# The order of the first loads and of the output stage's work in a gated pair of linear attentions

## The chip, the cores and the metric

The kernel runs on one core of a Trainium2 chip. A core has a matrix engine (TensorE, called PE in the profile), a vector engine (VectorE, DVE), an activation engine (ScalarE, ACT), a general engine (GpSimd, POOL) and a sequencer that mostly issues transfers (SyncE, SP). The engines run on their own and wait for one another through semaphores. PE reads the on-chip memory SBUF and writes the accumulation memory PSUM; transfers between the chip's main memory and SBUF (DMA) are issued by SP or ACT. The metric is the device time of one execution in microseconds (us), as the median of several runs.

## The reference

Two linear attentions with 32 heads of width 20 work on the same input x (2048 rows, 640 columns, bf16) with weights of their own, and a gate mixes the two outputs row by row:

```python
x = A_x
g = sigmoid((x * gate_w).sum(-1, keepdims=True))
a = attention(x, A_wqkv, A_wo)
b = attention(x, B_wqkv, B_wo)
return g * a + (1 - g) * b

def attention(x, wqkv, wo):            # per head: q, k, v are 2048 x 20
    q, k, v = split(x @ wqkv)
    pq, pk = phi(q), phi(k)            # phi(t) = (t + 1 if t > 0 else exp(t)) + 1e-6
    kv, z = pk.T @ v, pk.sum(rows)
    o = (pq @ kv) / (pq @ z + 1e-6)
    return merge_heads(o) @ wo
```

## The kernel before

In the text that follows A and B are the two attentions. The kernel never forms v. For each attention it computes k = x wk in 16 chunks of 128 rows (`k_chunk`, line 227), applies phi (`phi`, lines 214 to 223), and computes q transposed (`q_block`, `q_unit`, lines 274 to 295). Then G = xᵀ phi(k) gives kv as a product with wv, and kv times wo gives a matrix M of 640 by 640 (`g_all`, `kv_mm`, `m_mm`); the scaled phi(q) times M is one attention's output. M goes through main memory (`m_dram`) to change its layout. The sum over A and B of these products in the output stage is written as a two by two block product with seven products in place of eight, on sums and differences of blocks: the sums of the phi(q) blocks are `p_sums` (three kinds, 1, 2 and 4, for each of four parts of 256 rows) and those of M's blocks `m_sum` (0 to 3), all of them on DVE at line 519.

**The start.** The weights wkA come in five row blocks c of 128 by 640, 160 KB each (`load_wk`, line 120). The first two row blocks of x, 160 KB each, are loaded as they are (`load_x`, line 114) and turned by PE against an identity matrix (`x_transpose`, line 206), with DVE copying each from PSUM to xT in two pieces (line 209). The other rows of x are turned by the transfer itself (`x_turned`, line 117), and come after the first loads in SP's queue, with wqA between them (line 130). SP issues the first x block and wkA's blocks 0, 2 and 4; ACT issues gate_w, the second x block and blocks 1 and 3. ACT loads its table for the exponential when the first one is due (the row of line 214 named ACT_TABLE_LOAD).

POOL builds constants (identity, masks, spreading matrices; lines 135 to 156). PE runs seven products of 512 columns of ones into an unused bank (`warm`, line 163). The gate's logit is a 641st column of wkA: gate_w is loaded as 5 rows of 128 (`grow`), turned by PE (line 165), copied by DVE (`gsb`, line 167) and put by POOL into column 640 of each block of wkA (line 169, five copies). The products of a k chunk come in two halves of the columns; half 0 has 320 columns, half 1 has 321 with the gate's. `k_first` starts the first two chunks block by block: for each of the blocks 0, 1 and 2 both chunks with both halves, then blocks 3 and 4 of each chunk. POOL also clears R and fills parts of it from I16 (lines 686 to 691); this is used much later.

**The output stage.** Each of eight `Pair` objects i makes the output rows of row blocks i and i + 8. Its products p1 to p7 are five PE instructions of 320 columns each (`prod`, line 575). p1 and p5 go first for all pairs, in PSUM banks x and z, and ACT copies them into the memory of xn (lines 605, 609). p2 has the banks w and y; p6, p7 and p4 use bank x in this order: ACT copies p6's result (line 628), p7 accumulates on it, DVE adds that to an output tile, p4 accumulates further, DVE adds again. p3 has bank z. u25 (DVE) makes v out of p6's copy and p5; c11 (DVE) makes an output part of p2 and p1. DVE's additions are all at line 580, stores of finished rows at line 595, and the tiles for output rows are four in number. Where a product accumulates on a bank that DVE still has to read, PE waits.

**What sets the order.** Parts under `manual_schedule` run in the order of the program text on each engine; the rest is ordered by a planner. Every engine takes its own instructions strictly in order, and SP and ACT issue their transfers in the order of their instruction streams. In the kernel before, the first loads, the constants, the warm-ups and the gate column stand outside `manual_schedule`, `k_first` and the whole output stage inside.

Of the kernel before, what the change touches and what calls it, by code (L numbers as in the profile page):

```python
# [31 lines left out]
def kernel(  # L32
# [66 lines left out]
    lift = persist.tile([P, 1], FP32, name="lift")  # L99
# [5 lines left out]


    nc.vector.memset(ones[:], 1.0)
    nc.vector.memset(lift[:], 1.0 + EPS)
    wk = [None, None]
    wv = [None, None]  # L110
    wq = [None, None]
# [16 lines left out]
    x_turned(2 * P, HB)  # L128
    wq[0] = wpool.tile([P, DT, D], BF16, tag="wq", name="wqA")
    nc.sync.dma_start(out=wq[0][:], in_=wq_dram[0][:, :, 0:D])  # L130
    for n in range(1, NB):
        x_turned(n * HB, (n + 1) * HB)


    make_identity(nc, ident[:])
    for r in range(4):
        rows = slice(32 * r, 32 * r + 32)
        nc.gpsimd.tensor_copy(out=I4[rows], in_=ident[rows, rows])
    nc.gpsimd.tensor_copy(
        out=spread[:].rearrange("p (h t) -> p h t", t=TW), in_=I4[:, :, None].to_broadcast([P, H, TW])  # L140
    )
    nc.gpsimd.tensor_tensor(
        out=I16[0:2 * ST], in0=ident[0:2 * ST, 0:ST], in1=ident[0:2 * ST, ST:2 * ST], op=ALU.add
    )
    nc.gpsimd.memset(maskE[:], 1.0)
    for sign, base in ((1, 0), (-1, Dh - 1)):
        nc.gpsimd.affine_select(
            out=maskE[:], in_=maskE[:], pattern=[[-sign * Dh, WB[0] // Dh], [0, Dh]],
            compare_op=ALU.is_ge, fill=0.0, base=base, channel_multiplier=sign,
        )  # L150
    nc.gpsimd.memset(headE[:], 1.0)
    for sign, base in ((1, 0), (-1, TW - 1)):
        nc.gpsimd.affine_select(
            out=headE[:], in_=headE[:], pattern=[[-sign * TW, H]],
            compare_op=ALU.is_ge, fill=0.0, base=base, channel_multiplier=sign,
        )


    raw = ps_raw("warm", 3)
    warm = raw.bitcast(FP32).rearrange("p (b n) -> p b n", b=2)  # L160
    one_l, one_r = [nc.const_aps.tensor(1.0, [P, n], BF16) for n in (P, HB)]
    for k in range(7):
        nc.tensor.matmul(warm[:, 0, :], lhsT=one_l, rhs=one_r, start=True, stop=True)  # L163
    gcol = raw[:, 2 * HB:2 * HB + DT]
    nc.tensor.transpose(out=gcol, in_=grow, identity=ident[0:DT, 0:DT])
    gsb = work.tile([P, DT], BF16, tag="rT", name="gsb")
    nc.vector.tensor_copy(out=gsb[:], in_=gcol)
    for c in range(DT):
        nc.gpsimd.tensor_copy(out=wk[0][:, c, D:D + 1], in_=gsb[:, c:c + 1])

    def by_group(dst, lhsT, src, h):

# [31 lines left out]
    def x_transpose(i, pt, cuts=(0, DT)):  # L204
        for c in range(DT):
            nc.tensor.transpose(out=pt[:, c * P:(c + 1) * P], in_=xn[:, i, c * P:(c + 1) * P], identity=ident[:])
        src = pt[:, 0:D].rearrange("p (c n) -> p c n", c=DT)
        for lo, hi in zip(cuts, cuts[1:]):
            nc.vector.tensor_copy(out=xT[:, lo:hi, i * P:(i + 1) * P], in_=src[:, lo:hi])  # L209

    def phi(dst, src, n, lifted=False, side=None):

        e = work.tile([P, src.shape[1], n], BF16, tag="e", name="e", bufs=3)
        nc.scalar.activation(out=e[:], in_=src, func=ACT.Exp)  # L214
        if side is not None:
            side()
        if lifted:
            nc.scalar.activation(out=dst, in_=src, func=ACT.Identity, bias=lift[:])
# [462 lines left out]


    with tc.manual_schedule():
        k_first()
    turn[0] = 2
    nc.gpsimd.memset(R[:, :, 0:2, :], 0.0)
# [31 lines left out]
    with tc.manual_schedule():  # L718
# [35 lines left out]
        with late_pool("mid") as mid:  # L754
# [110 lines left out]
```

## Time and profile before

| | |
|---|---|
| median of 3 runs | 187.31 us (187.2 to 188.5) |
| profiled execution | 187.03 us, of which 185.3 us from the first to the last instruction (span) |
| PE busy | 181.4 us, 1338 products |
| DVE busy | 149.0 us |
| ACT busy | 78.6 us |
| POOL busy | 6.0 us |
| transferred | 17.59 MB, mean 95 GB/s |
| granted TensorE clock | 1.00 in the whole span |

All times in the text count from the start of the span unless they are whole executions. A PE row's length contains the time until the last result is in PSUM; the distance between the starts of two products tells the pace. An engine with a high busy share is not yet the bound: the chain of work that ended last tells which engine's work, or which wait, the end hangs on. A bracket at the end of a timeline row is the idle time of that engine before the row, and what ended it, as far as the semaphores tell.

### The profile page before, as it was taken

What the parts mean: (1) busy time and instruction counts of PE and PEld (TensorE: products, weight loads), DVE (VectorE), ACT (ScalarE), POOL (GpSimd) and SP (SyncE); (2) the same over time, 40 slices, a digit from 0 to 9 for tenths busy, and PEclk for the clock granted to TensorE, in tenths of its full rate; (3) what the DMA queues carried; (4) which work ended last, traced back from release to release, by engine and by line L of the source; (5) the groups of instructions that cost most, each with busy time, mean ns of one, the idle gap of its engine ahead of it and who ended that gap; (6) DMA issues with size and microseconds to landing.
All of it is one profiled execution on the core that took longest, in us unless ns stands there. A gap on an engine that the chain in (4) does not pass through costs nothing.

```text
span 185.3 us, 3375 instructions
## 1 busy us (share of the span) xinstructions
PE 181.4 (98%) x1338; PEld 121.6 (66%) x1338; DVE 149.0 (80%) x236; ACT 78.6 (42%) x132; POOL 6.0 (3%) x30
## 2 busy tenths in 40 slices
PE   8999999999999999999999999999999999999993
PEld 3666657755576677877765555576778777677762
DVE  0387869899999999799889998739699986978863
ACT  2345555557951501367664577431501863111010
POOL 6400000010000000000000000000000000000000
PEclk9999999999999999999999999999999999999999
DMA  5999998041140000011115000000533570023224
GB/s 166 332 240 165 308 372 189 6 132 46 19 162 0 0 4 0 0 36 34 55 45 189 4 0 0 0 4 0 177 89 92 175 182 3 35 106 110 108 83 131
DMA packets 21022, 17.59 MB, mean 95 GB/s; under 512 B 9998, under 2 KB 20750, under 8 KB 21006
## 3 DMA queue, kind: packets, MB, share of 16 engines
q1 hardware_dynamic: 20276, 16.72, 32.3%
q10 hardware_dynamic: 730, 0.66, 1.0%
q8 instruction: 10, 0.16, 0.4%
q14 instruction: 6, 0.05, 0.1%
HBM read 10.81 MB, written 4.26 MB: 81 GB/s over the span
## 4 chain that ended last, share of the span: by engine, by line
PE 97%; DVE 1%; issue 0%; ACT 0%
PE gs L351 17%; PE kA L227 12%; PE kB L227 12%; PE qB L274 12%; PE ox L575 11%; PE qA L274 6%; PE oz L575 6%; PE qA L285 5%; PE gB L324 2%; PE gA L324 2%; PE ow L575 2%; PE warm L163 2%; PE qA L295 1%; PE s L476 1%; PE mA L476 1%; PE kvA L446 1%
## 5 line engine op out<-in xcount | busy, mean ns | idle before, releaser
L227 PEld LDWEIGHTS <-xT 128*128 128x128 bf16 x320 | 31.1, 98 | 12.7 <-DVE xT L209 0.4
L219 DVE TENSOR_SCALAR e<-e 128x640 bf16<-128x640 bf16 (+2 forms) x53 | 18.9, 356 | 8.5 <-ACT e L214 7.9
L227 PE MATMUL kB<-wkB,xT 128*128 128x320 bf16 x160 | 23.0, 299 | 0.0
L227 PE MATMUL kA<-wkA,xT 128*128 128x320 bf16 (+1 forms) x160 | 22.6, 302 | 0.0
L274 PE MATMUL qB<-xT,wqB 128*128 128x512 bf16 x100 | 21.8, 379 | 0.0
L214 ACT ACTIVATE e<-kB 128x640 bf16<-128x640 f32 x16 | 11.3, 703 | 18.8 <-PE kB L227 17.5
L274 PEld LDWEIGHTS <-wqB 128*128 128x128 bf16 x100 | 11.7, 117 | 9.8 <-issue 0.2
L214 ACT ACTIVATE e<-kA 128x640 bf16<-128x640 f32 x16 | 11.2, 704 | 12.5 <-PE kA L227 12.5
L223 DVE SCALAR_TENSOR_TENSOR pk<-kA,e 128x640 bf16<-128x640 f32 x16 | 13.2, 825 | 2.1
L223 DVE SCALAR_TENSOR_TENSOR pk<-kB,e 128x640 bf16<-128x640 f32 x16 | 13.2, 825 | 1.7
L214 ACT ACTIVATE e<-qB 128x1024 bf16<-128x1024 f32 x10 | 10.2, 1023 | 8.7 <-PE qB L274 8.4
L214 ACT ACTIVATE e<-qA 128x1024 bf16<-128x1024 f32 (+1 forms) x11 | 10.4, 946 | 8.1 <-PE qA L285 5.1
L628 ACT COPY u<-ox 128x320 f32<-128x320 f32 x8 | 3.4, 425 | 20.2 <-PE ox L575 20.2
L351 PEld LDWEIGHTS <-S 128*128 128x128 bf16 x96 | 9.4, 98 | 3.6
L351 PEld LDWEIGHTS <-xn 128*128 128x128 bf16 x96 | 9.1, 98 | 4.0 <-issue 0.4
L274 PE MATMUL qA<-xT,wqA 128*128 128x512 bf16 x50 | 11.0, 379 | 0.0
L575 PEld LDWEIGHTS <-xT 128*128 128x128 bf16 x85 | 8.1, 98 | 3.2 <-issue 0.3
L575 PEld LDWEIGHTS <-pqTB 128*128 128x128 bf16 x80 | 7.8, 98 | 3.4 <-issue 0.2
L575 PEld LDWEIGHTS <-pqTA 128*128 128x128 bf16 x80 | 7.7, 98 | 3.1 <-DVE pqTA L519 0.3
L351 PE MATMUL gs<-pk,xn 128*128 128x320 bf16 x64 | 9.4, 300 | 0.0
L223 DVE SCALAR_TENSOR_TENSOR pqTB<-qB,e 128x1024 bf16<-128x1024 f32 x7 | 8.6, 1225 | 0.7
L274 PEld LDWEIGHTS <-wqA 128*128 128x128 bf16 x50 | 5.9, 117 | 4.8
(138 smaller groups left out, 287.0 us busy)
## 6 DMA issues: line engine op xcount, KB each, us to landing
out_dram<-osb SPq DMA_DIRECT2D x14, 160.0 KB, 1.8
xn<-in_A_x_dram SPq DMA_DIRECT2D x3, 640.0 KB, 5.6
wqA<-in_A_wqkv_dram SPq DMA_DIRECT2D x1, 800.0 KB, 5.1
wvA<-in_A_wqkv_dram SPq DMA_DIRECT2D x1, 800.0 KB, 10.1
wkB<-in_B_wqkv_dram SPq DMA_DIRECT2D x1, 800.0 KB, 4.8
wqB<-in_B_wqkv_dram SPq DMA_DIRECT2D x1, 800.0 KB, 4.5
MA<-mA_dram SPq DMA_DIRECT2D x1, 800.0 KB, 4.5
wvB<-in_B_wqkv_dram SPq DMA_DIRECT2D x1, 800.0 KB, 4.6
```

The source lines that it names most:

```text
L163: nc.tensor.matmul(warm[:, 0, :], lhsT=one_l, rhs=one_r, start=True, stop=True)
L214: nc.scalar.activation(out=e[:], in_=src, func=ACT.Exp)
L219: nc.vector.tensor_scalar(e[:], e[:], 1.0, EPS, op0=ALU.min, op1=ALU.add)
L223: nc.vector.scalar_tensor_tensor(out=dst, in0=src, scalar=1.0 + EPS, in1=e[:], op0=ALU.add, op1=ALU.max)
L227: nc.tensor.matmul(pt[:, hf, 0:w], lhsT=xT[:, c, i * P:(i + 1) * P], rhs=wk[b][:, c, hf * HF:hf * HF + w], start=(c == 0), stop=(c == DT - 1),
L274: nc.tensor.matmul(pt[:, u, :], lhsT=mixed(wq[b][:, c, :], m), rhs=xT[:, c, n * HB:(n + 1) * HB], start=(c == 0), stop=(c == DT - 1),)
L285: nc.tensor.matmul(pt[:, u, :], lhsT=mixed(wq[b][:, c, :], m + u), rhs=xT[:, c, n * HB:(n + 1) * HB], start=(c == 0), stop=(c == DT - 1),)
L324: nc.tensor.matmul(pt[:, hf, 0:HF], lhsT=xn[:, i, c * P:(c + 1) * P], rhs=pk[:, i, hf * HF:(hf + 1) * HF], start=(i == 0), stop=(i == ST - 1),
L351: nc.tensor.matmul(pt[:, n, 0:HF], lhsT=left[:, i, n * P:(n + 1) * P], rhs=right[:, i, :], start=(first and i == 0), stop=(i == hc - 1), s ...
L476: nc.tensor.matmul(dst[:w, 0:HF], lhsT=KVA[:w, k, 0:w], rhs=wo_sb[b][:w, k, n * HF:(n + 1) * HF], start=True, stop=True,)
L575: nc.tensor.matmul(dst, lhsT=left[:, c, r0:r0 + P], rhs=right[:, c, :], start=(first and c == 0), stop=(c == DT - 1), skip_group_check=not ...
L628: nc.scalar.copy(out=self.u6[:], in_=self.at("x"))
```

## The change

Four things are edited at the start. The second x block is loaded by SP, behind the first; wkA's blocks 0, 1 and 2 follow on SP, and blocks 3 and 4 are issued by ACT. ACT's queue now holds gate_w, then an exponential of one column (into a new second column of `lift`), for which the table is loaded, then the two blocks. The warm-ups are five products of 512 columns and two of 128. The gate column (transpose, DVE copy, POOL copies) comes after the turning of both x blocks, and within a chunk the products go by half first: half 0 of blocks 0 and 1, half 1 of both; then the other chunk; then block 2; then blocks 3 and 4. The loads and the constants are called inside `manual_schedule`; the clearing and filling of R stays outside it, and in the resulting order of POOL's instructions it stands between the constants, ahead of the five gate copies, where it stood behind them before.

In the output stage p1 of pairs 4 and 5 goes between p5 of pairs 1, 2 and 3; the sums 2 and 4 of a third part of rows are made before the inner loop instead of in it; m_sum(3) follows m_sum(2) directly, ahead of the c11 additions; and p3 of pair 6 stands between p7 of pair 6 and p6 of pair 7, where it was the product after p7 of pair 7. What PE computes in the two stages is the same, apart from the warm-ups.

```diff
-    nc.scalar.dma_start(out=grow, in_=gate_w.rearrange("(c p) -> c p", p=P))
-    load_x(nc.sync, 0)
-    load_x(nc.scalar, 1)
-    for c, eng in enumerate((nc.sync, nc.scalar, nc.sync, nc.scalar, nc.sync)):
-        load_wk(eng, c, c + 1)
...
+    def first_loads():
+
+        nc.scalar.dma_start(out=grow, in_=gate_w.rearrange("(c p) -> c p", p=P))
+        nc.scalar.activation(out=lift[:, 1:2], in_=lift[:, 0:1], func=ACT.Exp)
+        for i in range(2):
+            load_x(nc.sync, i)
+        for c in range(DT):
+            load_wk(nc.sync if c < 3 else nc.scalar, c, c + 1)
+        x_turned(2 * P, HB)
+        nc.sync.dma_start(out=wq[0][:], in_=wq_dram[0][:, :, 0:D])
+        for n in range(1, NB):
+            x_turned(n * HB, (n + 1) * HB)
...
-    for k in range(7):
-        nc.tensor.matmul(warm[:, 0, :], lhsT=one_l, rhs=one_r, start=True, stop=True)
...
+    def warm_up(n, w):
+        for k in range(n):
+            nc.tensor.matmul(warm[:, 0, 0:w], lhsT=one_l, rhs=one_r[:, 0:w], start=True, stop=True)
+
+    def gate_column():
+        nc.tensor.transpose(out=gcol, in_=grow, identity=ident[0:DT, 0:DT])
+        gsb = work.tile([P, DT], BF16, tag="rT", name="gsb")
+        nc.vector.tensor_copy(out=gsb[:], in_=gcol)
+        for c in range(DT):
+            nc.gpsimd.tensor_copy(out=wk[0][:, c, D:D + 1], in_=gsb[:, c:c + 1])
...
-        for i in range(2):
-            x_transpose(i, raw[i], (0, 2, DT))
-
-        def part(i, cs):
-            for c in cs:
-                for hf in range(2):
-                    k_mm(0, i, c, pts[i], hf)
-
-        for c in range(3):
-            for i in range(2):
-                part(i, (c,))
+        warm_up(5, HB)
+        warm_up(2, P)
+        x_transpose(0, raw[0], (0, 2, DT))
+        x_transpose(1, raw[1], (0, 2, DT))
+        gate_column()
+
+        def part(i, cs):
+            for hf in range(2):
+                for c in cs:
+                    k_mm(0, i, c, pts[i], hf)
+
+        part(0, (0, 1))
+        part(1, (0, 1))
+        for i in range(2):
+            part(i, (2,))
         for i in range(2):
             part(i, (3, 4))
             k_done(0, i, pts[i])
...
     with tc.manual_schedule():
+        first_loads()
+        constants()
         k_first()
...
-        for i in range(1, 4):
-            pairs[i].p5()
+        pairs[1].p5()
         for n in (2, 3):
             p_sums(part[n], (1,))
-        for i in range(4, half):
-            pairs[i].p1()
+        for i in (4, 6):
+            for k in range(2):
+                pairs[i + k].p1()
+                if i == 4:
+                    pairs[2 + k].p5()
         for i in range(4, half):
             pairs[i].p5()
-        for n in range(2):
+        for n in range(3):
             p_sums(part[n], (2, 4))
...
-        m_sum(1)
-        m_sum(2)
+        for k in (1, 2, 3):
+            m_sum(k)
...
-        m_sum(3)
-        later = {0: (2, (2,)), 1: (2, (4,)), 2: (3, (2,)), 3: (3, (4,))}
         ahead = {1: 4, 3: 5, 5: 6}
+        later = {1: 2, 3: 4}
         for i in range(half - 1):
             p, after = pairs[i:i + 2]
             p.p7()
             if i in ahead:
                 pairs[ahead[i]].p2()
                 pairs[ahead[i]].c11()
-            if i < half - 2:
-                p.p3()
+            p.p3()
             after.p6()
             after.u25()
             p.p4()
             if i in later:
-                p_sums(part[later[i][0]], later[i][1])
-        p, after = pairs[half - 2:]
+                p_sums(part[3], (later[i],))
         after.p7()
-        p.p3()
         after.p2()
         after.c11()
         after.p4()
         after.p3()
```

More of the change, by code (lines that the diff above doesn't have):

```diff
@@ L98 @@
     m_dram = [scratch.tile([D, D], BF16, name=f"m{b}_dram") for b in "AB"]
-    lift = persist.tile([P, 1], FP32, name="lift")
+    lift = persist.tile([P, 2], FP32, name="lift")
     TM = [persist.tile([P, DT, HF], BF16, name="TM0")] + [None] * 3
@@ L107 @@
     nc.vector.memset(ones[:], 1.0)
-    nc.vector.memset(lift[:], 1.0 + EPS)
+    nc.vector.memset(lift[:, 0:1], 1.0 + EPS)
     wk = [None, None]
@@ L122 @@
     grow, logitT = R[0:DT, 0, 2, 0:P], R[:, 0, 1, 0:P]
-    nc.scalar.dma_start(out=grow, in_=gate_w.rearrange("(c p) -> c p", p=P))
-    load_x(nc.sync, 0)
-    load_x(nc.scalar, 1)
-    for c, eng in enumerate((nc.sync, nc.scalar, nc.sync, nc.scalar, nc.sync)):
-        load_wk(eng, c, c + 1)
-    x_turned(2 * P, HB)
-    wq[0] = wpool.tile([P, DT, D], BF16, tag="wq", name="wqA")
-    nc.sync.dma_start(out=wq[0][:], in_=wq_dram[0][:, :, 0:D])
-    for n in range(1, NB):
-        x_turned(n * HB, (n + 1) * HB)
@@ L135 @@
[L135 to L149, printed above, removed]
-        )
@@ L151 @@
[L151 to L155, printed above, removed]
-        )
+    wq[0] = wpool.tile([P, DT, D], BF16, tag="wq", name="wqA")
+    def first_loads():
[9 more added lines that the diff above has]
+            x_turned(n * HB, (n + 1) * HB)
@@ new lines, in constants @@
+    def constants():
+        make_identity(nc, ident[:])
+        for r in range(4):
+            rows = slice(32 * r, 32 * r + 32)
+            nc.gpsimd.tensor_copy(out=I4[rows], in_=ident[rows, rows])
+        nc.gpsimd.tensor_copy(
+            out=spread[:].rearrange("p (h t) -> p h t", t=TW), in_=I4[:, :, None].to_broadcast([P, H, TW])
+        )
+        nc.gpsimd.tensor_tensor(
+            out=I16[0:2 * ST], in0=ident[0:2 * ST, 0:ST], in1=ident[0:2 * ST, ST:2 * ST], op=ALU.add
+        )
+        nc.gpsimd.memset(maskE[:], 1.0)
+        for sign, base in ((1, 0), (-1, Dh - 1)):
+            nc.gpsimd.affine_select(
+                out=maskE[:], in_=maskE[:], pattern=[[-sign * Dh, WB[0] // Dh], [0, Dh]],
+                compare_op=ALU.is_ge, fill=0.0, base=base, channel_multiplier=sign,
+            )
+        nc.gpsimd.memset(headE[:], 1.0)
+        for sign, base in ((1, 0), (-1, TW - 1)):
+            nc.gpsimd.affine_select(
+                out=headE[:], in_=headE[:], pattern=[[-sign * TW, H]],
+                compare_op=ALU.is_ge, fill=0.0, base=base, channel_multiplier=sign,
+            )
@@ L161 @@
     one_l, one_r = [nc.const_aps.tensor(1.0, [P, n], BF16) for n in (P, HB)]
-    for k in range(7):
-        nc.tensor.matmul(warm[:, 0, :], lhsT=one_l, rhs=one_r, start=True, stop=True)
     gcol = raw[:, 2 * HB:2 * HB + DT]
[L165 to L169, printed above, removed]
+    def warm_up(n, w):
[7 more added lines that the diff above has]
+            nc.gpsimd.tensor_copy(out=wk[0][:, c, D:D + 1], in_=gsb[:, c:c + 1])
     def by_group(dst, lhsT, src, h):
@@ L217, in phi @@
         if lifted:
-            nc.scalar.activation(out=dst, in_=src, func=ACT.Identity, bias=lift[:])
+            nc.scalar.activation(out=dst, in_=src, func=ACT.Identity, bias=lift[:, 0:1])
         nc.vector.tensor_scalar(e[:], e[:], 1.0, EPS, op0=ALU.min, op1=ALU.add)
```

## The prediction

> **What bounds it now.** I read the page first: engines, then the chain that ended last.
>
> ```profile
> PE 181.4 (98%) x1338; PEld 121.6 (66%) x1338; DVE 149.0 (80%) x236; ACT 78.6 (42%) x132; POOL 6.0 (3%) x30
> ...
> PE 97%; DVE 1%; issue 0%; ACT 0%
> ```
>
> TensorE (PE) is busy for 181.4 of 185.3 us and is 97% of the chain. The change removes no product of the calculation, so it can only win where PE works on nothing useful or waits: the first 6 us, a few stalls in the output stage, and the tail. Next the timeline of the first 16 us (start, length, engine, line, operation, and in brackets the idle time before it):
>
> ```profile
> 0.84 3.15 PE L163 MATMUL warm<-const-bfloat16-1.0 128*128 128x512 bf16 x7 [0.84 <-PEq L849]
> ...
> 3.61 0.20 POOL L153 TENSOR_SCALAR_AFFINE_SELECT headE<-headE 128x32 bf16<-128x32 bf16 x1
> ...
> 4.03 1.27 PE L206 MATMUL xt<-ident,xn 128*128 128x128 bf16 x10
> 4.14 0.16 DVE L167 COPY gsb<-warm 128x5 bf16<-128x5 bf16 x1 [3.16 <-PE warm L165]
> 4.37 0.66 POOL L169 COPY wkA<-gsb 128x1 bf16<-128x1 bf16 x5 [0.55 <-DVE gsb L167]
> 4.78 1.11 DVE L209 COPY xT<-xt 128x256 bf16<-128x256 bf16 x4 [0.48 <-PE xt L206]
> ...
> 4.96 0.95 POOL L686 MEMSET R<- 128x1024 bf16 x1
> ...
> 5.68 5.02 PEld L227 LDWEIGHTS <-xT 128*128 128x128 bf16 x38 [0.42 <-DVE xT L209]
> 5.97 0.98 POOL L691 COPY R<-I 32x128 bf16<-32x128 bf16 x4
> ```
>
> Warm-ups fill PE to 4.0 us, the ten transposes of x take 0.11 us each (4.03 to 5.13), and the first products of wkA start at 5.13. The third of them waits for VectorE's (DVE's) last copies of the transposed x (0.42 us before 5.68). My anchor is the fifth product: in narrow windows six start before 6.20, and the one still running at 6.20 began at 5.97. From there PE takes 0.136 us a product without a gap. Whatever moves that fifth product moves the end.
>
> The same view of the output stage shows the stalls there, as gaps before weight loads (PEld) and as the DVE operation that was late:
>
> ```profile
> 147.68 6.63 PEld L575 LDWEIGHTS <-pqTA 128*128 128x128 bf16 x50 [0.28 <-DVE pqTA L519]
> ...
> 158.67 0.98 DVE L519 TENSOR_TENSOR TM<-MB,TM 128x1600 bf16<-128x1600 bf16 x1
> ...
> 159.57 0.48 DVE L580 TENSOR_TENSOR osb<-ox,xn 128x320 bf16<-128x320 f32 x1
> ...
> 160.11 0.50 PEld L575 LDWEIGHTS <-pqTB 128*128 128x128 bf16 x4 [0.23 <-issue]
> ...
> 176.90 0.98 DVE L580 TENSOR_TENSOR osb<-ox,xn 128x320 bf16<-128x320 f32 x2
> ...
> 177.44 0.50 PEld L575 LDWEIGHTS <-xT 128*128 128x128 bf16 x4 [0.29 <-issue]
> ```
>
> Five products of 320 columns take 0.68 us (chain of waits). Measured against that, PE lost 0.11 us at 147.6, 0.18 at 159.9 to 160.1, 0.10 at 166.3 and 0.25 at 177.2 to 177.4: 0.64 us in all.
>
> **The start, part by part.** *Warm-ups.* Seven of 512 columns become five of 512 and two of 128: at 0.43 and 0.11 us each here, that is 0.86 - 0.22 = 0.64 us less, and PE is free at 0.84 + 2.3 = 3.1 instead of about 3.8. The first x block lands at 0.81 + 2.3 = 3.1, so its transposes start about 0.9 us earlier.
>
> *Gate column.* This is the step that decides. The gate's transpose (L165) and its DVE copy move behind the ten transposes and the four xT copies. By the instruction order, POOL's five copies into wkA (L169) move behind the memset of R and the four R copies, which stood after them before. POOL worked without a break on constants until 3.61 + 0.20 = 3.81; with 0.95 and 0.98 us put ahead, the gate copies cannot start before 5.74, and waits between dependent POOL operations, now interleaved differently, may make it 6.0. The first copy lasts 0.19 us; DVE to POOL took 0.07 us from end to start, so PE may go on at 6.0 to 6.25. What waits: the new order of parts gives half 0, blocks 0 and 1, then half 1 (321 columns, the last one being the gate), so two products can run early and the third waits for POOL. Behind it stands PE's whole queue. The DVE route says nearly the same: transposes of the second x end near 5.1, two copies of 0.3 us and the 0.16 us copy end near 5.9. The third product at 6.1 puts the fifth at 6.4, against 5.97: **+0.40 us** (0.3 to 0.55). The stall that goes (0.42 at 5.68) is inside this. The warm-ups' 0.64 us are thus used up waiting.
>
> *Loads.* The second x moves from ScalarE (ACT) to second place on SP; blocks 0, 1, 2 of wkA follow on SP; blocks 3 and 4 go to ACT behind gate_w's issue (to 1.38), the table load (1.28) and a one-column Exp. The trace has no such Exp: at least the 0.15 us of a one-column copy, at most the 0.70 of a 640-column Exp; I take 0.2, as the width is the copy's. Block 3 is then issued at 2.9 and block 4 at 3.4. Landing took 3.1 to 4.0 us after issue for the wkA blocks: 6.0 to 6.9 and 6.5 to 7.4. They are read by products 13 and 14, at 6.4 + 8 x 0.136 = 7.5 and 7.6. Covered; at the upper end by 0.2 us. Without that cover each 0.1 us late is 0.1 us on the end. The earlier table load is worth nothing: it lay at 2.76 to 4.04, and ACT's first Exp waits for PE until 7.81.
>
> On SP, everything behind moves one issue (0.46 us) later: the first x_turned from 2.68 to 3.14, wqA from 4.81 to 5.27. wqA landed 5.1 us after issue, so at 10.4, and is read from 10.74 + 0.4. x_turned is read by product 21, which was at 5.97 + 16 x 0.136 = 8.15. What is open is the pace of one queue:
>
> ```profile
> 2.50:3.00 0.50, 0.50 (x3) 0.21 (x2) 0.00 (x0) 0.24 (x1) 0.38 (x3) 1.00 0.76 141
> ...
> 4.00:4.50 0.50, 0.50 (x6) 0.46 (x6) 0.16 (x1) 0.04 (x1) 0.14 (x2) 1.00 0.98 351
> ...
> 8.00:8.50 0.50, 0.50 (x6) 0.37 (x4) 0.00 (x0) 0.50 (x3) 0.00 (x0) 1.00 1.04 371
> ```
>
> In these stretches the last column is GB/s. Before 3 us, when only SP's small loads were moving, it was 141; with ACT's beside them 351; in one large load of SP (wqA) 371. SP's four blocks landed at 3.1, 4.4, 5.3 and 5.8 (issues at 0.81, 1.27, 1.74, 2.20, and 2.3, 3.1, 3.6, 3.6 to landing); ACT's last at 6.3. The mean step of 0.9 us on one queue would land the second x at 4.0 to 4.4, blocks 0, 1, 2 at about 5.2, 6.1, 7.0, against reads at about 5, 5.3 and 7.2. Block 1 at 6.1 is as late as POOL, x_turned some 0.7 us later than before: up to 0.3 us more. At the shared pace of 0.53 a block (six blocks from 3.1 to 6.3) there is no cost. I take **+0.10 us** (0 to 0.9; the top is the rival below).
>
> The Trainium skill (DMA: Bandwidth & Descriptors, "Issuing engines are not separate DMA queues") says that several issuers only save issue time, since all run on the same 16 engines. By that rule one queue is no slower and this term is zero; the 141 against 351 GB/s above speaks against it for small loads, though the first stretch is also a start-up.
>
> **The output stage.** (a) p1 of pair 4 now stands between p5 of pairs 1 and 2, 0.68 us of cover for the sum of part 1: -0.11 (none to -0.11). (b) m_sum(3), 0.98 us of DVE, stood just ahead of p7's addition at 159.57. It moves ahead of the c11 additions, and two sums of 0.82 us fill DVE's 1.95 us wait for MB before 154.24. From 154.24 DVE runs three m_sums (0.9 apart), three c11, u25, c11 (0.4 apart) to about 159.0, so p7's addition ends at 159.4 and p4 at 159.9 finds it done: -0.18 (0 to -0.18). (c) In iteration 6 p3 moves between p7 and p6: 0.68 us of cover for the addition that PE waited 0.25 us for. But the last p4 loses one product of cover: p7's addition of pair 7 then ends about 0.05 us after p4 could start. -0.18 (+0.1 to -0.25). The 0.10 at 166.3 stays, as a sum still stands before that addition. Together **-0.47 us** (+0.1 to -0.55). The tail behind the last product is unchanged.
>
> **Sum.** The profiled execution took 187.03 us (span 185.3 and 1.7 around it). 187.03 + 0.40 + 0.10 - 0.47 = 187.06. The median of the runs shown is 187.31; I carry half of the 0.28 us between them: **187.2 us**, no change. The forecast's own range is 186.7 to 187.7.
>
> **Rivals.**
> *The gate copies are not late* (the change does what it says): POOL is done sooner than my sum or the first products come without waiting. For it: POOL rows are rough. Against: 1.93 us of rows stand ahead. The transposes then end at about 4.7, products start near 4.75 instead of 5.13 and lose no 0.3 us to DVE: about -0.4 instead of +0.5, so 186.3 us.
>
> *The clock rises late* (slower than before). Seven warm-ups took 0.43 us each and twenty products of the same width (qA) 0.216 each (4.32 in the chain), while the granted clock in the rows stays at 1.00: PE started at half pace, and at about 5.4 us its products went from 0.24 to 0.136 us. Before, PE had then been busy without a break for 4.5 us. Now it idles about 0.5 us for the second x and 1 us for POOL. If that puts the rise off to a time t, the products between 6.1 and t cost double: half of that time. One period more, as long as what was needed here at least (5.4 - 0.84 = 4.5 at most, some 3.4 if the first part did not count): t near 8.8, +1.35 us, 188.6; two, 190.3. It decides if the idle time falls below what counts as busy; the trace has no such gap to tell.
> The Trainium skill (TensorE: Matmul & The Clock Gate, Part 1) tells of a free-running window of about 3.4 us that must be busy before full clock; the trace agrees with the factor of two and the order of the time. By that rule the time of the rise also varies between executions, which would fit the runs of before (187.2 to 188.5), and the wait for POOL hides some of it.
>
> *One queue is slow.* With the largest step on SP (3.1 to 4.4, 1.25 us) or nearly it, blocks 1 and 2 land near 6.6 and 7.7, x_turned 1.5 us later than before: start +1.3, in all 187.03 + 1.3 - 0.47 = 187.9 to 188.2. For: 141 GB/s. Against: steps of 1.0 and 0.5 that followed.
>
> **Chances.** Forecast 0.57, gate copies in time 0.12, late clock 0.16, slow queue 0.15. Range 186.3 to 188.9: it leaves out half of the first rival and the late clock's upper part. One per cent is 1.87 us, about what a measurement here can tell from no change. No case reaches 185.4; 0.02 for what I do not see. Above 189.2 lies the late clock with two periods, or with one on top of a slow queue: 0.11. The rest, 0.87, is within 1%.
>
> **What would show it.** Right: POOL's copies into wkA near 5.8 to 6.0; PE idle for 0.5 to 1 us ending with them; two products before it; gaps at 147.6, 160 and 177.4 gone, a small one before the last p4. Wrong: products running without a wait at 5 us; spacings of 0.27 us after 6.1 (clock); a DMA of wkA or x_turned as the releaser of a PE wait; DVE late in a new place.

## The result, and the profile after

The changed kernel took 189.03 us (median of 22 executions, 187.22 to 190.89), the kernel before, on the same chip, 187.36 us (22, 186.79 to 189.89). The ratio is 1.0054, 95% interval 1.0034 to 1.0074: slower by half a per cent. It leaves out executions more than 1.5% above a kernel's fastest (three of the changed kernel, one of the kernel before), and it is not the quotient of the medians, which is 1.0089. The forecast of 187.2 us was wrong, and 189.03 lies just above its range.

The times of the changed kernel stand in three clusters: five at 187.2 to 187.6, fourteen at 188.4 to 189.7, three at 190.3 to 190.9. Their medians are 187.4, 189.1 and 190.8, so steps of about 1.7 us. The kernel before has 18 of its 22 executions below 187.9.

The profiled execution took 188.61 us (span 186.9), in the middle cluster. The two lines of its page that answer to those of before, busy time and the chain that ended last:

```profile
PE 181.8 (97%) x1333; PEld 122.5 (66%) x1338; DVE 149.3 (80%) x236; ACT 78.9 (42%) x133; POOL 6.0 (3%) x30
...
PE 91%; DMA 3%; DVE 2%; SPq 1%; issue 1%; ACT 0%; DVEq 0%
```

TensorE is still the bound, but the chain now has 3% of DMA, 2% of VectorE and 1% of SP's issuing in it, which before were 0 or 1%. The timeline of the start of the changed kernel shows where (start, length, engine, line, operation; in brackets the idle time before, and its end):

```profile
1.41 1.28 ACT L128 ACT_TABLE_LOAD   x1 [1.41 <-PEq L861]
1.47 0.84 ACTq L120 DMA_DIRECT2D wkA<-in_A_wqkv_dram  x2
...
1.73 1.37 SPq L120 DMA_DIRECT2D wkA<-in_A_wqkv_dram  x3
...
3.14 1.33 PE L214 MATMUL xt<-ident,xn 128*128 128x128 bf16 x10
...
4.40 0.18 PE L173 MATMUL warm<-ident,R 5*128 5x5 bf16 x1
...
5.17 0.43 PE L235 MATMUL kA<-wkA,xT 128*128 128x320 bf16 x1 [0.59 <-DVE gsb L175]
...
5.71 0.65 POOL L177 COPY wkA<-gsb 128x1 bf16<-128x1 bf16 x5
5.89 7.02 PE L235 MATMUL kA<-wkA,xT 128*128 128x320 bf16 x39 [0.30 <-DMA wkA<-in_A_wqkv_dram]
...
12.76 1.46 PE L297 MATMUL qA<-xT,wqA 128*128 128x512 bf16 x5
```

PE begins to turn x at 3.14, done at about 4.3, and then has almost nothing: one gate transpose, one product at 5.17 when wkA's block 0 is there (landed 5.13; the bracket names DVE's gate copy, which ended at the same time), one at 5.89 with block 1 (landed 5.85). The third product, the first that reads the gate column, starts at 6.11, where before it started at 5.69. POOL is not what held it: its first gate copy ran from 5.71 to 5.89, which would have let the third start at about 5.94 (with blocks 3 and 4 held, below, it started 0.05 us after that copy), and it came 0.22 us behind the second, the same distance as in the run below whose gate copies were long done. So block 1 set it.

The largest item stands in no bracket: 38 products from the third to the first of qA took 10.88 - 5.69 = 5.19 us before and 12.76 - 6.11 = 6.65 after. The first of qA before:

```profile
10.88 4.48 PE L285 MATMUL qA<-xT,wqA 128*128 128x512 bf16 x20
```

A table by microsecond of the first wkA products shows why. Columns: stretch, its length, PE's busy time with the number of products that ran in it (one that crosses an edge counts in both stretches), the clock as the profile has it, DMA share, GB/s. First before:

```profile
6.00:7.00 1.00, 1.00 (x9) 1.00 1.24 279
7.00:8.00 1.00, 1.00 (x9) 1.00 1.02 333
8.00:9.00 1.00, 1.00 (x10) 1.00 1.04 366
```

And the changed kernel:

```profile
6.00:7.00 1.00, 1.00 (x5) 1.00 0.84 135
7.00:8.00 1.00, 1.00 (x6) 1.00 1.13 267
8.00:9.00 1.00, 1.00 (x5) 1.00 1.02 335
9.00:10.00 1.00, 1.00 (x8) 1.00 1.08 337
10.00:11.00 1.00, 1.00 (x10) 1.00 1.61 96
```

PE is fully busy in both, yet five or six products run in a microsecond until about 9 us and nine or ten at the later pace; in single records the distance from start to start is 0.267 us, then 0.136. This is half pace. The clock column says 1.00 throughout, here as for the kernel before, but that is no measurement of the start: the trace's own clock events begin with full clock from 9.09 us on (5.73 before), and the column shows 1.00 where there is no event. The recorded lengths of full clock are 177.49 us here and 180.91 before; they differ by 3.42 us and are 52 and 53 times 3.41.

In the output stage DVE's rows of the changed kernel around the one larger stall that is left:

```profile
162.73 0.98 DVE L592 TENSOR_TENSOR osb<-ox,xn 128x320 bf16<-128x320 f32 x2
165.18 0.49 DVE L592 TENSOR_TENSOR osb<-ow,xn 128x320 bf16<-128x320 f32 x1 [1.47 <-DMA out_dram<-osb]
...
166.79 0.81 DVE L531 TENSOR_TENSOR xT<-pqTA 128x1280 bf16<-128x1280 bf16 x1
167.52 0.48 DVE L592 TENSOR_TENSOR osb<-ox,xn 128x320 bf16<-128x320 f32 x1
```

and the weight loads of PE that waited for the last of them:

```profile
168.06 0.50 PEld L587 LDWEIGHTS <-pqTB 128*128 128x128 bf16 x4 [0.32 <-issue]
```

DVE stood idle for 1.47 us, since c11 of pair 4 writes into one of the four output tiles, and the store that had it landed only then. Behind it four additions, the sum at 166.79 and the addition at 167.52 came late, and p4's second part waited 0.28 us more than its pace (0.10 at this place before). The stalls at 147.6, 160 and 177.4 are gone; one of 0.065 us stands before the last p4. In all the output stage lost 0.35 us, against 0.65.

The sum closes: 187.03 (profiled before) + 0.43 (third product) + 1.45 (half pace) - 0.30 (output) = 188.61, in one pair of profiles.

### The profile page after: what moved, and what is told of

Same layout as the page of the kernel before. It is cut to its first block, busy times and chain, and to the rows that moved or that the text cites. A ratio compares the mean times of both kernels' runs of the same rounds, so it can differ in the third digit from the quotient of the medians.

```text
span 186.9 us, 3369 instructions
## 1 busy us (share of the span) xinstructions
PE 181.8 (97%) x1333; PEld 122.5 (66%) x1338; DVE 149.3 (80%) x236; ACT 78.9 (42%) x133; POOL 6.0 (3%) x30
## 4 chain that ended last, share of the span: by engine, by line
PE 91%; DMA 3%; DVE 2%; SPq 1%; issue 1%; ACT 0%; DVEq 0%
PE gs L363 17%; PE kA L235 13%; PE kB L235 12%; PE qB L286 12%; PE ox L587 10%; PE qA L286 6%; PE oz L587 5%; PE qA L297 5%; PE gB L336 2%; PE gA L336 2%; DMA wkA<-in_A_wqkv_dram 2%; PE ow L587 2%; DVE osb L592 1%; PE qA L307 1%; DMA out_dram<-osb 1%; PE s L488 1%
## 5 line engine op out<-in xcount | busy, mean ns | idle before, releaser
L235 PEld LDWEIGHTS <-xT 128*128 128x128 bf16 x320 | 31.8, 100 | 14.3 <-issue 1.2
L235 PE MATMUL kA<-wkA,xT 128*128 128x321 bf16 (+1 forms) x160 | 24.1, 313 | 0.9 <-DVE gsb L175 0.6
L222 ACT ACTIVATE e<-qA 128x1024 bf16<-128x1024 f32 (+1 forms) x11 | 10.4, 946 | 8.1 <-PE qA L297 5.1
L587 PEld LDWEIGHTS <-xT 128*128 128x128 bf16 x85 | 8.1, 98 | 2.9
```

Source lines behind the costliest of these rows:

```text
L235: nc.tensor.matmul(pt[:, hf, 0:w], lhsT=xT[:, c, i * P:(i + 1) * P], rhs=wk[b][:, c, hf * HF:hf * HF + w], start=(c == 0), stop=(c == DT - 1),
L587: nc.tensor.matmul(dst, lhsT=left[:, c, r0:r0 + P], rhs=right[:, c, :], start=(first and c == 0), stop=(c == DT - 1), skip_group_check=not ...
```

## The experiments

**Theories.** *Clock*: PE's pauses around 5 us put off the rise of its pace, and this is the larger half of the loss. *POOL*: the late gate copies make the pause. *Loads*: the new order of loads makes it, whatever POOL does. Each run has its median with the number of executions, the median of before on the same chip, and the ratio with its interval. None changes what the kernel computes; where products of ones are added or dropped, nothing reads them.

### The two halves of the change

The changed kernel with the output stage put back as it was before, so that only the start differs from the kernel before:

```diff
-        pairs[1].p5()
+        for i in range(1, 4):
+            pairs[i].p5()
         for n in (2, 3):
             p_sums(part[n], (1,))
...
```

> Only the start of the change; the output stage as before. In the two profiles the start costs 1.87 us on PE's stream and the output stage gives 0.30 back. Both theories below say about 189.3 us, 0.3 above the whole change (189.0). If it is at or below the change, the output edits give nothing.

189.91 us (4 executions, 188.19 to 190.72), before 187.53; 1.0112 (1.0068 to 1.0157). The profiled execution was its fastest, 188.19 us. Its PE timeline:

```profile
6.24 0.30 PE L235 MATMUL kA<-wkA,xT 128*128 128x320 bf16 x1 [1.58 <-DMA wkA<-in_A_wqkv_dram]
6.73 5.47 PE L235 MATMUL kA<-wkA,xT 128*128 128x320 bf16 x39 [0.19 <-DMA wkA<-in_A_wqkv_dram]
```

Block 0 landed at 6.20 here, 1.1 us later than in the changed kernel's profile; the pace was already full at 6.73, and the trace's first clock event has full clock from 4.64 us on, ahead of the pause, which did not take it back. So the start alone holds the loss, in two forms: wait for the block, or half pace. How the slower executions, up to 190.72 us, divide between them no profile shows. The start is that of the changed kernel, and up to 4.4 us PE's work in the two profiles agrees within 0.1 us: what differs is when the clock rose, 4.64 against 9.09.

The output stage alone, with the start as before:

```diff
-        for i in range(1, 4):
-            pairs[i].p5()
+        pairs[1].p5()
         for n in (2, 3):
             p_sums(part[n], (1,))
...
```

> Only the output stage of the change; the start as before. The gaps of PE in the output stage added up to 0.65 us before and 0.35 us in the change, so 0.30 us less than before: about 187.05. If the stores or the tail take it back, 187.35.

187.03 us (12), before 187.53; 0.9970 (0.9953 to 0.9988). The profiled execution took 186.70 us and its output stage lost 0.34 us. This half of the change is a gain, of 0.3 us by the gaps and 0.5 by the medians.

### Is it the clock?

Three products of 512 columns of ones fill PE between the turning of x and the gate's transpose, in the changed kernel:

```diff
         x_transpose(1, raw[1], (0, 2, DT))
+        warm_up(3, HB)
         gate_column()
```

> The whole change, with three more products of 512 columns of ones on PE between the turning of x and the gate's transpose (1.28 us at half pace): PE has no pause up to 5.6 us, but the first product of wkA comes at 5.7 and the third at about 6.2, 0.05 us later than in the change. Theory clock (a pause of PE delays the rise of its pace): the products after 6.2 run at 0.136 us, 1.4 us are won back, profiled about 187.2, median about 187.2. Theory wait (the loads and the gate column themselves cost the time): no gain, 189.0 to 189.1.

187.85 us (11, 187.50 to 188.15), before 187.53; 1.0014 (1.0003 to 1.0026). PE's timeline:

```profile
4.34 0.70 PE L214 MATMUL xt<-ident,xn 128*128 128x128 bf16 x5 [0.46 <-DMA xn<-in_A_x_dram]
4.85 0.84 PE L170 MATMUL warm<-const-bfloat16-1.0 128*128 128x512 bf16 x3
5.63 0.17 PE L173 MATMUL warm<-ident,R 5*128 5x5 bf16 x1
5.73 5.91 PE L235 MATMUL kA<-wkA,xT 128*128 128x320 bf16 x40
```

The three products started 0.25 and 0.22 us apart, so the pace had doubled at about 4.9 us, and the wkA products follow at 0.136. PE works on more, its third wkA product comes later (6.31 against 6.11), and the kernel is 1.2 us faster than the changed one; the two upper clusters are gone. This is the clearest run for the clock. The first clock event agrees: full clock from 4.90 us on. It still does not reach the kernel before: the third product comes 0.62 us later than there (here POOL's first gate copy, done at 6.26, does hold it, by 0.20 us), and wqA, which landed at 11.75 us, leaves a gap of 0.31 us ahead of the first qA product. (The longer distance behind that product, 11.79 to 12.26, is a product whose record is missing: its weight load stands at 12.04. The whole qA block is only 0.03 us longer than before.) The output stage lost 0.44 us here, 0.10 of it waiting for M of B, so 0.21 less than before: 187.03 + 0.62 + 0.34 - 0.21 = 187.78, and the profiled execution took 187.79.

From the other side, the kernel before with the changed kernel's warm-ups:

```diff
-    for k in range(7):
-        nc.tensor.matmul(warm[:, 0, :], lhsT=one_l, rhs=one_r, start=True, stop=True)
+    for w in (HB,) * 5 + (P,) * 2:
+        nc.tensor.matmul(warm[:, 0, 0:w], lhsT=one_l, rhs=one_r[:, 0:w], start=True, stop=True)
```

> The kernel before with the change's warm-ups alone (five of 512 columns and two of 128). PE waits near 3.8 for the second x block, which lands at 4.5 as before: a pause of about 0.7 us and nothing else is later. If a pause of that length is enough to delay the rise of the pace, many executions cost 1.3 us more: 188.5. If it takes a longer one (the change has about 1.2 us in two pieces), 187.5.

187.90 us (12), before 187.47; 1.0027 (1.0001 to 1.0053): seven executions at 187.2 to 187.9, five at 188.2 to 189.0. The profiled one, 188.45 us, is of the upper kind, and its timeline has the pause:

```profile
5.03 0.72 PE L206 MATMUL xt<-ident,xn 128*128 128x128 bf16 x5 [0.92 <-DMA xn<-in_A_x_dram]
```

The second x block landed at 4.98 (4.54 before), when PE was through with the first at 3.9 (4.54 before); half pace then lasted to 8.19. So dropping 0.64 us of products that nobody reads costs 0.4 us in the median, in a kernel in which nothing else is touched; the lower end of the interval is close to no change.

And the kernel before with three warm-ups in all:

```diff
-    for k in range(7):
+    for k in range(3):
```

> The kernel before with three warm-ups instead of seven: 1.7 us less of PE work that computes nothing, all loads and orders as before. PE waits for the x blocks (3.1 and 4.5) and the first product still comes at about 5.1. Theory clock: PE is idle for about 1.7 us of the first 5, the rise comes a period later in all or nearly all executions, 1.2 to 1.7 us more: 188.6 to 189.2. Theory wait: nothing but the loads sets the start, 187.4.

189.74 us (4), before 187.56; 1.0118 (1.0058 to 1.0177). The profiled execution took 190.78 us. Its PE timeline has three pauses, and the table by microsecond half pace until 12.0:

```profile
3.24 0.71 PE L206 MATMUL xt<-ident,xn 128*128 128x128 bf16 x5 [0.84 <-DMA xn<-in_A_x_dram]
4.86 0.72 PE L206 MATMUL xt<-ident,xn 128*128 128x128 bf16 x5 [0.91 <-DMA xn<-in_A_x_dram]
...
7.60 5.66 PE L227 MATMUL kA<-wkA,xT 128*128 128x320 bf16 x25 [0.92 <-DMA wkA<-in_A_wqkv_dram]
```

```profile
9.00:10.00 1.00, 1.00 (x6) 1.00 1.12 311
10.00:11.00 1.00, 1.00 (x5) 1.00 1.04 352
```

PE's queue had no gap after 7.60 and was slow for about 4.3 us more; the first clock event is at 11.89. The third pause is not the warm-ups' alone: block 1 landed at 7.55 here, 5.57 before, with the same order of loads. So this profile shows more than the price of the warm-ups; the fastest of the four executions, 188.25, is 0.7 us above the median of before.

### POOL or the loads?

POOL's part is undone: the gate column goes ahead of the turning of x, as before, and R behind the gate copies.

```diff
+        gate_column()
         x_transpose(0, raw[0], (0, 2, DT))
         x_transpose(1, raw[1], (0, 2, DT))
-        gate_column()
...
         k_first()
+        nc.gpsimd.memset(R[:, :, 0:2, :], 0.0)
...
     turn[0] = 2
-    nc.gpsimd.memset(R[:, :, 0:2, :], 0.0)
...
```

> The whole change, but the gate column ahead of the turning of x, as before, and the clearing and filling of R on POOL behind the gate copies, as before. POOL's copies are then done near 4.9. If POOL was what PE waited for, the pause is gone and the time is 187.0. If the loads of blocks 0 and 1 of wkA (landing at 5.13 and 5.85 in the change) hold PE as well, the pause stays, the third product starts at about 6.0 and the time is 188.9.

189.09 us (12), before 187.53; 1.0067 (1.0038 to 1.0095): no better than the changed kernel. The first wkA product in the profile, 189.56 us:

```profile
6.16 7.05 PE L235 MATMUL kA<-wkA,xT 128*128 128x320 bf16 x35 [1.52 <-DMA wkA<-in_A_wqkv_dram]
```

With all five gate copies done at 5.08 PE waits 1.52 us for block 0 (landed 6.12), and half pace lasts to 10.3. POOL does not make the pause; the blocks of wkA are late without it. PE's pause is about as long as that of the start alone (1.58 us), but there the clock had risen before it; here full clock begins at 10.28.

The loads alone, in the kernel before:

```diff
-    load_x(nc.scalar, 1)
-    for c, eng in enumerate((nc.sync, nc.scalar, nc.sync, nc.scalar, nc.sync)):
-        load_wk(eng, c, c + 1)
+    nc.scalar.activation(out=lift[:, 1:2], in_=lift[:, 0:1], func=ACT.Exp)
+    load_x(nc.sync, 1)
+    for c in range(DT):
+        load_wk(nc.sync if c < 3 else nc.scalar, c, c + 1)
```

> The kernel before with the change's first loads alone (order and queues, and the early Exp); seven warm-ups, gate column, order of parts and output stage as before. In the change ACT issued blocks 3 and 4 at 1.47 and 1.87, ahead of SP's block 0 at 1.73. Theory loads (blocks 0 and 1 come late because 3 and 4 go first): blocks 0 and 1 land at 5.1 to 6.2 and 5.9 to 6.7 as in the change, PE waits about 0.5 us or more, 188 to 189.5. Theory rest (the waits come from the gate column or the warm-ups): blocks in time, 187.4.

187.83 us (12, 187.12 to 189.78), before 187.47; 1.0023 (0.9992 to 1.0054), which cannot be told from no change. The profiled execution took 188.53 us. Its pace rose in time: seven warm-ups lead up to block 0 (landed 5.28). It lost later, as the waits between 8 and 16 us show (total, how often, longest):

```profile
PE qA L286 <- DMA wqA<-in_A_wqkv_dram: 1.3, 1, 1.3
```

wqA landed at 12.26, 7.3 us after its issue (9.86 and 5.1 before). So here the loads did not put off the clock, with seven warm-ups ahead of them. The loads alone cost 0.2% and the fewer warm-ups alone 0.3%; the start with both costs 1.1%, and where the gate column was as before and the gain of the output stage was in it, the sum was 0.7%. Added up, the two alone give 0.5%; the start with the gate column as before costs 1.0%, when the 0.3% of the output stage is added back. That the two together cost more than their sum is likely by this, but the intervals, 0.3% to each side, do not show it. One edit was not tested alone: the new order of products needs block 1 for the second product, where the order before needs it for the fifth, so it leaves PE one product of cover, not four, while that block is late. Across the profiles block 0 landed at 4.1 to 4.7 us in the five with the old order of loads, and at 5.1 to 6.2 in the five with the changed one; the changed kernel's PE is through with x at 4.3, 0.8 us sooner than before.

### Blocks 3 and 4 held back

In the changed kernel's timeline ACT issues blocks 3 and 4 at 1.47 and 1.87 us, while its table is still loading (1.41 to 2.69). The prediction had them at 2.9 and 3.4. Here they are held there: each block's issue waits for an exponential that writes the gate's place in it, a column that POOL overwrites later.

```diff
-        nc.scalar.activation(out=lift[:, 1:2], in_=lift[:, 0:1], func=ACT.Exp)
+        for c in (3, 4):
+            nc.scalar.activation(out=wk[0][:, c, 0:1], in_=lift[:, 0:1], func=ACT.Exp)
```

> The whole change, but the early Exp is done twice and writes a first column of blocks 3 and 4, so that their loads wait for it and are issued near 3.1 instead of 1.47. Theory loads: block 0 lands near 4.5 and block 1 near 5.2; the third product still waits for POOL's copy at 5.9, so the fifth starts near 6.2, and PE pauses 0.7 us in all instead of about 1.2: between 187.3 (the clock rises in time) and 188.9 (late), both more evenly than in the change. Theory one queue (SP's small loads are slow by themselves): block 0 still at 5.1 or later, 189.

188.72 us (6, 188.49 to 188.94), before 187.47; 1.0076 (1.0064 to 1.0089). ACT's rows in the profile (188.49 us):

```profile
1.40 1.28 ACT L129 ACT_TABLE_LOAD   x1 [1.40 <-PEq L862]
2.69 0.30 ACT L129 ACTIVATE wkA<-lift 128x1 bf16<-128x1 f32 x2
2.93 0.84 ACTq L120 DMA_DIRECT2D wkA<-in_A_wqkv_dram  x2
```

The blocks now leave at 2.93 and 3.40. Blocks 0, 1 and 2 land at 5.07, 5.55 and 6.95, against 5.13, 5.85 and 6.79 in the changed kernel, and half pace lasts to 9.08 as there. Whether ACT's early blocks hold back block 0 is left open: this pair differs by 0.06 us, but block 0 landed at 5.07 and 4.81 in the two profiles with blocks 3 and 4 held, and at 5.13 to 6.20 in the five with them early. Here POOL's first copy, done at 5.88, did hold the third product, by 0.12 us. The same with POOL's part undone too:

```diff
-        nc.scalar.activation(out=lift[:, 1:2], in_=lift[:, 0:1], func=ACT.Exp)
+        for c in (3, 4):
+            nc.scalar.activation(out=wk[0][:, c, 0:1], in_=lift[:, 0:1], func=ACT.Exp)
...
+        gate_column()
         x_transpose(0, raw[0], (0, 2, DT))
         x_transpose(1, raw[1], (0, 2, DT))
-        gate_column()
...
```

> Blocks 3 and 4 held behind the Exp, and gate column and R as before on POOL: the change without its two waits. Theory loads: first product near 4.6, fifth at 5.3 to 5.6, no pause of PE above 0.4 us, clock in time: 186.6 to 186.9, faster than before. Theory one queue: blocks 0 to 2 at 5.1 or later, 188.5 to 189.

189.28 us (6), before 187.47; 1.0101 (1.0079 to 1.0124). PE's timeline:

```profile
4.85 0.43 PE L236 MATMUL kA<-wkA,xT 128*128 128x320 bf16 x1 [0.21 <-DMA wkA<-in_A_wqkv_dram]
5.48 3.37 PE L236 MATMUL kA<-wkA,xT 128*128 128x320 bf16 x12 [0.20 <-DMA wkA<-in_A_wqkv_dram]
9.76 2.49 PE L236 MATMUL kA<-wkA,xT 128*128 128x320 bf16 x17 [0.90 <-DMA wkA<-in_A_wqkv_dram]
```

Block 0 came at 4.81 and block 1 at 5.44, the brackets show two pauses of only 0.2 us, and the products still run at half pace to 8.4 at least; then the held-back block 4 is late by 0.9 us. (A bracket counts from the end of the last result. From start to start, less a product's pace, the two pauses are about 0.4 us each.) So with ACT's loads behind its table load and nothing of POOL in the way, the change was no faster; block 4, which is late only because it is held, is part of that.

### Versions made from the parts

The kernel before with the changed output stage, and the sums of the last part of rows made one iteration earlier, so that none stands behind DVE's wait for a store:

```diff
-        later = {1: 2, 3: 4}
+        later = {0: 2, 2: 4}
```

> The start as before, the output stage of the change, and the two sums that stay in its loop moved one iteration (after pairs 0 and 2 instead of 1 and 3). In the change the sum after pair 1 came 0.28 us late for p4 of pair 2, because DVE had just waited for a store; after pair 0 DVE idles in that wait anyway. Expected: the 0.28 us gap goes, 0.3 us below the output stage alone, about 0.55 to 0.6 us below the kernel before: 186.8. If the gap only moves to another pair: 187.05.

186.90 us (12), before 187.56; 0.9967 (0.9942 to 0.9992), 0.3% faster than the kernel before; two of the twelve executions took 189.2 and 189.3. The profiled execution took 186.75 us. DVE's rows around the store:

```profile
161.54 0.82 DVE L519 TENSOR_TENSOR xT<-pqTA 128x1280 bf16<-128x1280 bf16 x1
162.28 0.49 DVE L580 TENSOR_TENSOR osb<-ox,xn 128x320 bf16<-128x320 f32 x1
163.60 0.49 DVE L580 TENSOR_TENSOR osb<-ow,xn 128x320 bf16<-128x320 f32 x1 [0.84 <-DMA out_dram<-osb]
```

The sum now lies ahead of the wait, the wait is 0.84 in place of 1.47 us, and the only gap left in the output stage is 0.066 us before the last p4. Against the output edits alone (187.03) the further gain is within the scatter; the gaps say 0.27 us. In this profile the pace rose, by the spacing, only at about 6.4 us, with the start of the kernel before and no pause of PE. That cost 0.29 us, and the gaps of the output stage give 0.58: 187.03 + 0.29 - 0.58 = 186.74.

A start from both: x blocks and wkA's blocks 1 and 3 on SP, gate_w and blocks 0, 2 and 4 on ACT, gate column first, R behind it, the old order of products, the changed warm-ups, with that output stage:

```diff
         for c in range(DT):
-            load_wk(nc.sync if c < 3 else nc.scalar, c, c + 1)
+            load_wk(nc.sync if c % 2 else nc.scalar, c, c + 1)
...
```

> First loads in order of need, but over both queues: SP gets both x blocks and blocks 1 and 3, ACT gate_w and blocks 0, 2 and 4; gate column and order of parts as before; the change's warm-ups; output stage as in the kernel beside this. Theory loads and clock: block 0 lands near 4.5, block 1 near 5.2, the fifth product starts at 5.4 to 5.7 instead of 5.97, PE's pauses stay under 0.4 us, clock in time: 186.4 to 186.6. If those small pauses already delay the clock, 188 or more in most executions.

187.03 us (12), before 187.56; 0.9983 (0.9954 to 1.0012). Nine executions lie at 186.4 to 187.5 and three at 188.5 to 189.6, among these the profiled one (188.63 us):

```profile
4.61 0.72 PE L213 MATMUL xt<-ident,xn 128*128 128x128 bf16 x5 [0.50 <-DMA xn<-in_A_x_dram]
```

One pause of 0.50 us for the second x block, and half pace to 10.19. Two queues bring the common case back to the level of the best version, but with short warm-ups it stays exposed to one late load.

## Why the prediction was wrong

**The step that failed** is the choice between the forecast and its rival "the clock rises late". The forecast's sum let PE take 0.136 us a product from the fifth product on and had no term for a later rise of the pace; that term measured 1.45 us. The prediction named the mechanism, saw 0.5 us of idle time for the second x and 1 us for POOL, put t near 8.8 and the price at 1.35 us, and gave it 0.16, since the trace of before had no such gap to tell. (It read the rise of before as 5.4 from the spacing; the clock event has 5.73.) The runs have it: t = 9.09 and 1.45 us in the profile, 14 of 22 executions in that cluster, and three a further 1.7 us up, near what the rival gave for two periods (no profile shows one of these three). In the place of "decides if the idle time falls below what counts as busy" the runs put an estimate. The Trainium skill (TensorE: Matmul & The Clock Gate, Part 1) gives a free-running window of 3.4 us that must be busy; the clock events above, multiples of 3.41 us, agree, and the steps between the clusters, about 1.7 us, are half of such a period. So the window that ends at a rise sufficed, and the one before it did not. By the starts in the records, each product counted with its length at the pace of the time, PE was busy for an estimated 64% of the window that failed in the changed kernel (2.26 to 5.67), 67% with blocks 3 and 4 held, 68% with the five and two warm-ups in the kernel before (no clock event there; the rise is taken at 8.15 from the spacing), and 75% in the two-queue version; the windows that sufficed had 80% (filled), 87% (start alone, 1.23 to 4.64) and 89% (before). So by this estimate, from one profile of each, the bound lies near 80%: 0.7 us of idle time in a window passed, 0.9 failed. With that, the 1.5 us of the rival would have made 188.6 the likeliest time.

**Gate copies**: their time was right, the first copy at 5.71 where the prediction had not before 5.74, but they were not what PE waited for. The +0.43 at the third product agrees with the +0.40 by luck: POOL alone would have given about 0.25 (5.94 against 5.69), and block 1, landing at 5.85, gave the whole. The prediction had block 1 at 6.1, and let it count only as late as POOL.

**Loads**: the term of +0.10 was too small, since the 0.43 is theirs. Blocks 0, 1 and 2 were expected at 5.2, 6.1 and 7.0 and landed at 5.13, 5.85 and 6.79. The step for ACT was wrong: "Block 3 is then issued at 2.9" takes it that ACT's transfers wait for its own table and Exp; they left at 1.47 and 1.87. So for ACT's transfers it does not hold that an engine takes everything strictly in the order of its program. With the blocks held back, SP's five blocks landed at 3.19 to 6.95, 0.94 us apart (0.96 with POOL's part undone too), which is the 0.9 assumed for a queue of its own. The Trainium skill's rule (DMA: Bandwidth & Descriptors, "Issuing engines are not separate DMA queues"), by which it makes no difference who issues, would have had 0.53 there. The two profiles do not show a slow queue, though: between 2 and 4 us, with SP's loads alone moving, 213 to 325 GB/s went through in them, and the last of the five had ACT's blocks and the later transfers of x beside it. The 141 GB/s that the prediction took for SP's queue is one half microsecond; the one before it, 2.0 to 2.5 us, had 277. What the loads vary by was underrated: block 0 at 5.1 to 6.2 in the same order, and wqA, put at 10.4, landed at 10.7 to 12.3 there. In the changed kernel (11.43) this was hidden, as the products were later still; in the filled kernel it cost 0.34 us.

**The rival "one queue is slow"** (187.9 to 188.2): the profiled execution of the start alone took 188.19 us, with block 0 at 6.20 and blocks 1 and 2 at 6.68 and 7.11 (6.6 and 7.7 in the rival). It lacks the gain of the output stage, so it would be about 187.9 with it. One execution of this kind is shown, and not that the queue made it.

**Output stage**: -0.47 predicted, -0.30 measured. Three gaps went as expected and the new one before the last p4 was 0.065 (about 0.05 predicted). The term that was mis-sized is "The 0.10 at 166.3 stays": it became 0.28, since DVE's wait for a store now ended 1.6 us before the sum, and pushed it.

**Half of the 0.28 us** between profile and median: with the later runs the median of before was 187.36 to 187.56, so the whole of it would have been nearer.

**What stays open**: why small loads in one order land up to 1.1 us apart from one execution to the next, and why wqA takes 5.1 to 7.4 us from its issue; and what of the single queue's pace is the queue, what the transfers beside it. That the same kernel falls in one cluster or another by where the clock's window lies is borne out by one pair, the start alone and the changed kernel (4.64 and 9.09 us with the same start); no run sets that place.

## What to carry to other kernels

Warm-ups are not waste until the pace has doubled: count PE's busy share up to the moment when the data come, and shorten them only by what real work fills. When PE's rows look full but a stage has become longer, compare the distances between the starts of like products before looking for a wait. A step that removes one late arrival should be checked against the next one to arrive: here block 1 landed at 5.85 and POOL's first copy was done at 5.89.

## What was not expected of the hardware

- The pace of PE was half for up to 12.0 us of the span (three warm-ups), with a clock column of 1.00 in every row; the spacing, 0.267 against 0.136 us for 320 columns, and the first clock event of the trace, at 11.89, show it.
- ACT issued two transfers at 1.47 and 1.87 us with its own table load running from 1.41 to 2.69 and an Exp ahead of them in its order; only a true dependency (the exponential writing into the block) held them, to 2.93.
- A pause of 0.50 us in the first 5 us of PE (two-queue version) was followed by half pace to 10.19; that execution took 188.63 us, 1.6 above the median of its kernel. One of 1.58 us behind the rise at 4.64 (the start alone) left the pace full.
